# A decode-attention kernel loads V with 64 KB runs, one load per group, and computes its group weights in one block ahead of V's sums

## The chip, the cores and the metric

The kernel runs on one core of one Trainium2 chip. The metric is the device time of one execution in microseconds (us). Times below are medians of all runs of one kernel, with the lowest and the highest in brackets. A run is labelled slow when it lies more than 1.5% above the fastest of its kernel, and fast otherwise; ratios of times use fast runs alone. The profile is one execution; its span is some 1.5 us shorter than the measured time, and all moments in it count from the span's start.

## The reference

Two attention layers, A and B, each decode one token. Both have 32 query heads, 16 key/value heads and a head size of 128. A looks at the last 2048 positions of its cache, B at all 8192. The two outputs are concatenated.

```python
W = min(4096, max(256, Sk // 4))              # A: 2048 of 8192 positions; B uses all
q = (x @ wq).reshape(B, Sq, Hq, Dh)           # x is 1 x 576
scores = einsum("bhqd,bhkd->bhqk", q, k) * Dh ** -0.5
p = softmax(scores); o = einsum("bhqk,bhkd->bhqd", p, v)
out = o.reshape(B, Sq, Hq * Dh) @ wo
```

Every cache row and every weight is read once and used for one token. The input that must be moved is 102.8 MB.

## The kernel before

The work is cut into five groups: group 0 is all of A, groups 1 to 4 are four key/value heads of B each. On-chip memory has four slots of 4 MB, two for K and two for V. One engine (SyncE) issues all large loads in order, each after the work that last used its slot. The loads are carried out by 16 DMA engines, in packets; a packet here is one partition's contiguous run of memory (the packet records hold 2048 packets of 32 KB for B's K and V, 64 MB). TensorE does the matrix products, VectorE elementwise work and reductions, ScalarE the exponential. TensorE runs the groups in one hardware loop: it turns K by transposes, multiplies it with q, turns the softmax numerators P, and multiplies them with V.

V comes in two loads of two heads. Even and odd partitions hold different heads, and each partition's run of memory is 128 rows of 256 bytes, 32 KB:

```python
def load_kv(arrs, g, s, off, res, name):
    dst = slots[:, off:off + SLOT]
    def go(sp):
        if g:                                  # B: groups 1 to 4
            i = 4 * (g - 1) + 2 * s            # two heads
            return sp.dma_start(dst, arrs[1][0, i:i + 2, :, :].rearrange("e (p t) d -> p e (t d)", t=128))
        ...                                    # A: four loads with 8 KB runs
```

P is written twice next to each other by the exponential (for the two heads), turned, and masked by parity:

```python
# exponential: 512 scores -> 1024 columns
src = bass.AP(tensor=sacc, offset=0, ap=[[512, 128], [1, 512], [0, 2]])
act.activation(psb[:, :].rearrange("p (x g) -> p x g", g=2), src, ACT.Exp, bias=..., scale=SCALE, accum_out=...)
# turn: 8 transposes of 128 columns; then two masked copies of 512 columns on VectorE
for e in range(2):
    dve.tensor_scalar(to_e, turned_e, par2[:, e:e + 1], None, ALU.mult)
```

Each group then has 32 matmuls per V slot. In the last group, the chain that finds the weights of all groups (maximum, exponential, totals, scaling, combination; a ping-pong of TensorE, VectorE and ScalarE) stands between quarters of these sums:

```python
softmax_transpose(g, 18)
if last: weights_top(g)
v_slot(g, 0, 0, 20)
if last: weights_exp(g)
v_slot(g, 0, 1, 20.2)
if last: weights_sum(g)
v_keep(g, 0)
v_slot(g, 1, 0, 21)
if last: combine(range(NG - 1), ...); o_columns(0)
v_slot(g, 1, 1, 21.5)
v_keep(g, 1)
```

After the loop, the output weights of A (4.6 MB) and B (in four pieces, the last three in V's place) are multiplied with the result.

Of the kernel before, what the change touches and what calls it, by code (L numbers as in the profile page):

```python
# [12 lines left out]
DH = 128  # L13
# [5 lines left out]
NG = 5  # L19
# [17 lines left out]
class Program:  # L37
# [94 lines left out]
    def waits_of_loop(self, ops):  # L132
# [9 lines left out]
        for key, places in points.items():  # L142
# [26 lines left out]
            if len(fixed) == len(places):  # L169
                for place, hi in fixed.items():  # L170
# [4 lines left out]
                   for n in (1, 2, 16, 64) for first in (0, n) if fits(first, n, some, taker)]  # L175
# [100 lines left out]
def bass_concat_heads__sliding_block_cached__gqa_block_cached__decode_kernel(  # L276
# [24 lines left out]

    prog = Program(nc)
# [4 lines left out]
    ptm = nc.alloc_sbuf_tensor("ptm", [128, 1024], BF16)  # L307
    psb = nc.alloc_sbuf_tensor("psb", [128, 1024], BF16)
# [14 lines left out]
    maskV = nc.alloc_sbuf_tensor("maskV", [128, 8], F32)  # L323
# [3 lines left out]
    wlast = nc.alloc_sbuf_tensor("wlast", [128, 8], F32)  # L327
    vtmp = nc.alloc_sbuf_tensor("vtmp", [128, 8, DH], F32)
# [8 lines left out]
    opsum = nc.alloc_psum_tensor("opsum", [128, 1024], F32)  # L337
# [3 lines left out]
    B_O = [("bank", 5), ("bank", 6)]  # L341
    B_M = ("bank", 7)

# [3 lines left out]
    VS = [[("v", 0, 0), ("v", 0, 1)], [("v", 1)]]  # L347
    koff = lambda s: s * SLOT
    voff = lambda s: (2 + s) * SLOT
# [44 lines left out]
    def load_kv(arrs, g, s, off, res, name):  # L394
        dst = slots[:, off:off + SLOT]

        def go(sp):
            if g:
                i = 4 * (g - 1) + 2 * s
                return sp.dma_start(dst, arrs[1][0, i:i + 2, :, :].rearrange("e (p t) d -> p e (t d)", t=128))  # L400
            for m in range(4):
                i = 4 * m + 2 * s
                src = arrs[0][0, i:i + 2, SK - W_A:, :].rearrange("e (p t) d -> p e (t d)", t=32)
                ins = sp.dma_start(dst[:, m * UNIT:(m + 1) * UNIT], src)
                if m < 3:
                    op.also.append((16, ins))
            return ins
        op = add("sp", go, writes=res, dma="%s%d" % (name, s), inc=64)
# [19 lines left out]
    def q_part(P, off, res):  # L428
        def mm(pe):
            for u in range(9):  # L430
                for j in range(4):
                    o = off + u * 2048 + j * 512
                    ins = pe.matmul(opsum[32 * j:32 * j + 32, P * 512:(P + 1) * 512], lhsT=xpad[:, P, u, :],  # L433
                                    rhs=slots[:, o:o + 512], start=(u == 0), stop=(u == 8))
            return ins
        add("pe", mm, reads=[("xpad", P)] + res, writes=[B_O[P]])

    def q_finish(P):
        add("act", lambda act: act.activation(qrow[:, :], opsum[:, P * 512:(P + 1) * 512], ACT.Copy),  # L439
            reads=[B_O[P]], writes=["qrow"])  # L440

# [63 lines left out]
    def softmax_exp(g):  # L505
# [6 lines left out]
        def go(act):  # L512
            src = bass.AP(tensor=sacc, offset=0, ap=[[512, 128], [1, 512], [0, 2]])
            return act.activation(psb[:, :].rearrange("p (x g) -> p x g", g=2), src, ACT.Exp, bias=st(C_NB + g),  # L514
                                  scale=SCALE, accum_out=st(C_L + g))
# [3 lines left out]
    def softmax_transpose(g, place):  # L519
        dst = misc[:, :].bitcast(BF16)  # L520

        def tr(pe):
            for t in range(8):
                ins = pe.matmul(dst[:, t * 128:(t + 1) * 128], lhsT=psb[:, t * 128:(t + 1) * 128], rhs=ident[:, :],  # L524
                                start=True, stop=True, is_transpose=True)
            return ins
        add("pe", tr, reads=["psb", "ident"], writes=[B_M], loop=(g, place, None))

        def put(dve):
            for e in range(2):  # L530
                to = ptm[:, :].rearrange("p (n e y) -> p n e y", e=2, y=2)[:, :, e, :]
                src = dst.rearrange("p (n e y) -> p n e y", e=2, y=2)[:, :, e, :]
                ins = dve.tensor_scalar(to, src, par2[:, e:e + 1], None, ALU.mult)  # L533
            return ins
        add("dve", put, reads=[B_M, "par2"], writes=["ptm"], tag="put")


    def v_slot(g, s, half, place):
        v = slots[:, voff(s):voff(s) + SLOT].rearrange("p (m y) -> p m y", m=4)

        def mm(pe):
            for tt in range(4 * half, 4 * half + 4):
                for j in range(4):
                    o = tt * 128 + 32 * j
                    b = (8 * j + tt) * 128
                    ins = pe.matmul(opsum[32 * j:32 * j + 32, s * 512:(s + 1) * 512], lhsT=ptm[:, o:o + 32],  # L546
                                    rhs=v[:, :, b:b + 128], start=(tt == 0), stop=(tt == 7), skip_group_check=True)
            return ins
        add("pe", mm, reads=["ptm"] + VS[s], writes=[B_O[s]], loop=(g, place, None))


    def v_keep(g, s):
        last = g == NG - 1
        w = "wlast" if last else "maskV"
        by = bass.AP(tensor=wlast if last else maskV, offset=4 * s, ap=[[8, 128], [1, 4], [0, DH]])
        src = opsum[:, s * 512:(s + 1) * 512].rearrange("p (m d) -> p m d", m=4)
        add("dve", lambda dve: dve.tensor_tensor(vtmp[:, 4 * s:4 * s + 4, :], src, by, ALU.mult),  # L557
            reads=[B_O[s], w], writes=[("vtmp", s)], tag="keep")
        if s:
            sums((accs if last else acc)[:, g, :], vtmp[:, :, :].rearrange("p m d -> p d m"), [("vtmp", 0), ("vtmp", 1)],  # L560
                 [("accs" if last else "acc", g)], "keep")
# [4 lines left out]
    def weights_top(g):  # L566
        def turn(pe):
            pe.matmul(misc[0:1, 0:128], lhsT=st(C_M), rhs=identf[:, :], start=True, stop=True)  # L568
            return pe.matmul(misc[0:4, 128:256], lhsT=st(C_M + 1, 4), rhs=identf[:, :], start=True, stop=True)  # L569
# [181 lines left out]
```

## Time and profile before

| | before |
|---|---|
| time, us | 246.96 (246.78 to 247.31, 6 runs) |
| span of the profiled run, us | 245.4 |
| large loads (queue 1), packets | 5628 |
| sum of packet times, over 16 engines, us | 241.09 |
| packets of 8 KB, of 32 KB: mean time, ns | 313.4, 1217.8 |
| TensorE busy | 67% |

The lines below are from the page of the kernel before. The first four divide the span into 40 slices: the busy share of TensorE in tenths, its granted clock in tenths of full speed, the busy share of the DMA engines, and what they moved. The last line is the queue of the large loads: packets, MB, and the share of 16 engines' span that the packets took.

```profile
PE   0006329993836999443999390999671699859684
...
PEclk9999957999575999795899866599979599975679
DMA  9998999999999999999999999999999999999993
GB/s 349 421 445 383 426 425 421 418 418 419 469 419 433 438 423 427 427 438 427 427 434 443 438 433 433 427 427 427 433 433 427 433 438 433 427 445 427 403 416 140
...
q1 hardware_dynamic: 5628, 102.77, 98.2%
```

The DMA engines are busy almost throughout, while TensorE has gaps in every group. The kernel is bound by its loads (102.87 MB at a mean of 419 GB/s over the span). In the packet records, one packet follows another on an engine without a gap, from 1.0 us to the last weights.

These are the last pieces of the chain that ended last in the kernel before (start, length, what):

```profile
223.79 0.33 SPq L391
224.12 0.04 issue
224.16 18.52 DMA slots<-in_B_wo_dram
...
242.72 0.64 PE ktps L640 x16
...
243.39 0.31 DVE outsb L648
```

The 18.5 us are not a slow load: it is the wait in a full queue. After the last landing only 16 matmuls, a copy and the store are left.

This is TensorE and its helpers in the last group, from the timeline of the kernel before (start, length, engine, line, operation; in brackets the idle time before it and what ended it):

```profile
192.10 5.96 PE L472 MATMUL ktps<-ident,slots 128*128 128x128 bf16 x64 [6.88 <-PEq L214]
...
213.73 0.64 PE L493 MATMUL sacc<-kt,qst 128*32 128x512 bf16 x8 [0.37 <-PEq L214]
...
217.32 0.88 DVE L533 TENSOR_SCALAR ptm<-misc,par 128x512 bf16<-128x512 bf16 x2 [2.03 <-PE misc L524]
...
229.22 1.87 PE L546 MATMUL opsum<-slots,ptm 128*32 128x512 bf16 x13
...
231.86 1.87 DVE L384 TENSOR_REDUCE accs<-vtmp 128x128 f32<-128x1024 f32 x1
...
234.07 6.95 PE L640 MATMUL ktps<-slots,opj 128*32 128x288 bf16 x146
...
241.67 0.62 PE L640 MATMUL ktps<-slots,opj 128*32 128x144 bf16 x28 [0.65 <-DMA slots<-in_B_wo_dram]
242.72 0.61 PE L640 MATMUL ktps<-slots,opj 128*32 128x144 bf16 x16 [0.43 <-DMA slots<-in_B_wo_dram]
```

K's first half lands at 192.1; the last scores end at 214.4, V's sums at 231.1, and TensorE reaches the output weights of B only 0.65 us before their next piece lands. So in this run the tail of TensorE was nearly as late as the loads.

### The profile page before, as it was taken

What the parts mean: (1) busy time and instruction counts of PE and PEld (TensorE: products, weight loads), DVE (VectorE), ACT (ScalarE), POOL (GpSimd) and SP (SyncE); (2) the same over time, 40 slices, a digit from 0 to 9 for tenths busy, and PEclk for the clock granted to TensorE, in tenths of its full rate; (3) what the DMA queues carried; (4) which work ended last, traced back from release to release, by engine and by line L of the source; (5) the groups of instructions that cost most, each with busy time, mean ns of one, the idle gap of its engine ahead of it and who ended that gap; (6) DMA issues with size and microseconds to landing.
All of it is one profiled execution on the core that took longest, in us unless ns stands there. A gap on an engine that the chain in (4) does not pass through costs nothing. (4 is left out here: it accounts for less than half of the span.)

```text
span 245.4 us, 5175 instructions
## 1 busy us (share of the span) xinstructions
PE 165.1 (67%) x2285; PEld 117.5 (48%) x2285; DVE 87.2 (36%) x148; ACT 87.4 (36%) x95; POOL 10.7 (4%) x48
## 2 busy tenths in 40 slices
PE   0006329993836999443999390999671699859684
PEld 0002129781316876213877130978330687625463
DVE  0001205654142465250556323355524256533311
ACT  2000016873003786101778200577600378610000
POOL 7400000000000000000000000000000000000000
PEclk9999957999575999795899866599979599975679
DMA  9998999999999999999999999999999999999993
GB/s 349 421 445 383 426 425 421 418 418 419 469 419 433 438 423 427 427 438 427 427 434 443 438 433 433 427 427 427 433 433 427 433 438 433 427 445 427 403 416 140
DMA packets 5796, 102.87 MB, mean 419 GB/s; under 512 B 794, under 2 KB 924, under 8 KB 1180
## 3 DMA queue, kind: packets, MB, share of 16 engines
q1 hardware_dynamic: 5628, 102.77, 98.2%
q8 instruction: 5, 0.08, 0.1%
q10 hardware_dynamic: 160, 0.00, 0.0%
q14 instruction: 3, 0.02, 0.0%
HBM read 102.76 MB, written 0.00 MB: 419 GB/s over the span
## 5 line engine op out<-in xcount | busy, mean ns | idle before, releaser
L478 ACT ACTIVATE kt<-ktps 128x1024 bf16<-128x1024 bf16 x80 | 78.5, 1022 | 95.1 <-PE ktps L472 94.9
L472 PE MATMUL ktps<-ident,slots 128*128 128x128 bf16 x1280 | 89.1, 236 | 34.1 <-PEq L214 34.1
L472 PEld LDWEIGHTS ktps<-ident,slots 128*128 128x128 bf16 x1280 | 83.2, 107 | 49.7 <-issue 49.7
L481 DVE COPY kt<-ktps 128x1024 bf16<-128x1024 bf16 x80 | 55.3, 692 | 74.1 <-PE ktps L472 74.1
L546 PE MATMUL opsum<-slots,ptm 128*32 128x512 bf16 x320 | 32.0, 557 | 5.1 <-PEq L214 5.1
L493 PE MATMUL sacc<-kt,qst 128*32 128x512 bf16 x320 | 25.4, 392 | 1.9 <-PEq L214 1.9
L546 PEld LDWEIGHTS opsum<-slots,ptm 128*32 128x32 bf16 x320 | 13.0, 127 | 18.9 <-issue 16.8
L557 DVE TENSOR_TENSOR vtmp<-opsum,maskV 128x512 f32<-128x512 f32 x8 | 5.5, 692 | 22.6 <-PE opsum L546 22.6
L415 PE MATMUL misc<-xnine,twice 64*128 64x18 bf16 x1 | 0.2, 173 | 17.8 <-DMA xnine<-in_B_x_dram 17.8
L524 PE MATMUL misc<-ident,psb 128*128 128x128 bf16 x40 | 3.3, 230 | 11.6 <-PEq L214 11.6
L462 POOL COPY qst<-qcol 128x8 bf16<-128x8 bf16 x20 | 3.1, 191 | 163.7 <-PE sacc L493 149.3
L439 ACT ACTIVATE qrow<-opsum 128x512 bf16<-128x512 f32 x2 | 1.2, 597 | 22.7 <-PE opsum L433 22.7
L524 PEld LDWEIGHTS misc<-ident,psb 128*128 128x128 bf16 x40 | 2.5, 101 | 14.0 <-issue 14.0
L640 PE MATMUL ktps<-slots,opj 128*32 128x144 bf16 (+1 forms) x192 | 8.3, 271 | 1.1 <-DMA slots<-in_B_wo_dram 1.1
L514 ACT ACTIVATE psb<-sacc,stat 128x1024 bf16<-128x1024 f32 x5 | 5.6, 1114 | 9.5 <-DVE stat L508 9.5
L493 PEld LDWEIGHTS sacc<-kt,qst 128*32 128x32 bf16 x320 | 5.0, 94 | 7.9 <-issue 4.3
L415 PEld LDWEIGHTS misc<-xnine,twice 64*128 64x128 bf16 x1 | 0.1, 103 | 17.8 <-issue 17.8
L533 DVE TENSOR_SCALAR ptm<-misc,par 128x512 bf16<-128x512 bf16 x10 | 4.4, 480 | 10.4 <-PE misc L524 10.4
L640 PEld LDWEIGHTS ktps<-slots,opj 128*32 128x32 bf16 x192 | 6.2, 104 | 3.1 <-DMA slots<-in_B_wo_dram 1.5
L384 DVE TENSOR_REDUCE acc<-vtmp 128x128 f32<-128x1024 f32 x4 | 7.5, 1872 | 0.1
L433 PE MATMUL opsum<-slots,xpad 128*32 128x512 bf16 x72 | 6.2, 504 | 1.7 <-DMA slots<-in_B_wq_dram 0.9
L424 DVE TENSOR_SCALAR xpad<-misc,par 128x5 bf16<-128x5 f32 (+1 forms) x8 | 1.2, 230 | 14.0 <-PE misc L415 14.0
(65 smaller groups left out, 41.2 us busy)
## 6 DMA issues: line engine op xcount, KB each, us to landing
slots<-in_B_k_cache_dram SPq DMA_DIRECT2D x8, 4096.0 KB
slots<-in_B_v_cache_dram SPq DMA_DIRECT2D x8, 4096.0 KB
slots<-in_A_k_cache_dram SPq DMA_DIRECT2D x8, 1024.0 KB
slots<-in_A_v_cache_dram SPq DMA_DIRECT2D x8, 1024.0 KB
slots<-in_A_wq_dram SPq DMA_DIRECT2D x1, 4608.0 KB, 13.6
slots<-in_B_wq_dram SPq DMA_DIRECT2D x1, 4608.0 KB, 23.7
slots<-in_A_wo_dram SPq DMA_DIRECT2D x1, 4608.0 KB, 19.2
slots<-in_B_wo_dram SPq DMA_DIRECT2D x1, 3024.0 KB, 26.0
```

The lines of the kernel that those rows point to most:

```text
L384: add("dve", lambda dve: dve.tensor_reduce(out, view, AX.X, ALU.add), reads=reads, writes=writes, tag=tag)
L433: ins = pe.matmul(opsum[32 * j:32 * j + 32, P * 512:(P + 1) * 512], lhsT=xpad[:, P, u, :], rhs=slots[:, o:o + 512], start=(u == 0), stop=( ...
L472: ins = pe.matmul(ktps_bf[q][:, t * 128:(t + 1) * 128], lhsT=slots[:, o:o + 128], rhs=ident[:, :], start=True, stop=True, is_transpose=True)
L478: add("act", lambda act, q=q, dst=dst: act.activation(dst, ktps_bf[q], ACT.Copy), reads=[("bank", q)], writes=[("kt", u % NKT, q)], tag="e ...
L481: add("dve", lambda dve, q=q, dst=dst: dve.tensor_copy(dst, ktps_bf[q]), reads=[("bank", q)], writes=[("kt", u % NKT, q)], tag="e%d%d" % ( ...
L493: ins = pe.matmul(sacc[32 * j:32 * j + 32, :], lhsT=qst[:, o:o + 32], rhs=rhs, start=(u == 0 and e == 0), stop=True, skip_group_check=True)
L514: return act.activation(psb[:, :].rearrange("p (x g) -> p x g", g=2), src, ACT.Exp, bias=st(C_NB + g), scale=SCALE, accum_out=st(C_L + g))
L524: ins = pe.matmul(dst[:, t * 128:(t + 1) * 128], lhsT=psb[:, t * 128:(t + 1) * 128], rhs=ident[:, :], start=True, stop=True, is_transpose= ...
L533: ins = dve.tensor_scalar(to, src, par2[:, e:e + 1], None, ALU.mult)
L546: ins = pe.matmul(opsum[32 * j:32 * j + 32, s * 512:(s + 1) * 512], lhsT=ptm[:, o:o + 32], rhs=v[:, :, b:b + 128], start=(tt == 0), stop=( ...
L557: add("dve", lambda dve: dve.tensor_tensor(vtmp[:, 4 * s:4 * s + 4, :], src, by, ALU.mult), reads=[B_O[s], w], writes=[("vtmp", s)], tag=" ...
L640: ins = pe.matmul(ktps[P][32 * j:32 * j + 32, 0:w], lhsT=opj[:, P, jj:jj + 32], rhs=slots[:, o:o + w], start=(jj == 0), stop=(jj == HQ - 1))
```

## The change

The intent is longer packets. V of four heads comes in one 8 MB load, with partition 4p+h holding 256 rows of head h, a run of 64 KB. For this, P has to be spread over four heads instead of two and sorted by even and odd rows of K, which doubles P: the exponential writes 2048 columns, 16 transposes turn them, and two masked copies of 1024 columns follow. V's 64 sums run as one block into one bank, and what is kept afterwards is half as large. The weights chain of the last group goes, as one block, ahead of V's sums. A's V still has packets of 8 KB.

```diff
+    def load_v(g):
+        dst = slots[:, VOFF:VOFF + 2 * SLOT]
+        def go(sp):
+            if g:
+                return sp.dma_start(dst, vs[1][0, 4 * g - 4:4 * g, :, :].rearrange("h (p t) d -> p h (t d)", t=256))
+            for i in range(8):                                    # A
+                m, c = divmod(i, 2)
+                src = vs[0][0, 4 * m:4 * m + 4, SK - W_A:, :].rearrange("h (p c t) d -> p h c (t d)", c=2, t=32)[:, :, c, :]
 ...
-            src = bass.AP(tensor=sacc, offset=0, ap=[[512, 128], [1, 512], [0, 2]])
+            src = bass.AP(tensor=sacc, offset=0, ap=[[512, 128], [2, 256], [1, 2], [0, 4]])
+            dst = bass.AP(tensor=psb, offset=0, ap=[[2048, 128], [4, 256], [1024, 2], [1, 4]])
 ...
+            return dve.tensor_tensor(ptm[:, c * 1024:(c + 1) * 1024]..., dst..., mask, ALU.mult)   # once per c
 ...
+            for c in range(2):
+                for tt in range(8):
+                    for j in range(4):
+                        o = c * 1024 + tt * 128 + 32 * j
+                        b = (8 * j + tt) * 128
+                        ins = pe.matmul(opsum[32 * j:32 * j + 32, :], lhsT=ptm[:, o:o + 32], rhs=v[:, c, :, b:b + 128],
+                                        start=(c == 0 and tt == 0), stop=(c == 1 and tt == 7), skip_group_check=True)
 ...
-        (weights_top, v_slot, weights_exp, v_slot, weights_sum, v_keep, v_slot, combine, v_slot, v_keep)
+        for c in range(2):
+            softmax_transpose(g, c, 18 + c / 2)
+        if g == NG - 1:
+            weights_top(g)
+            weights_exp(g)
+            weights_sum(g)
+            combine(range(NG - 1), (g, 19.3, LAST))
+            o_columns(0)
+        v_sums(g, 20)
+        v_keep(g)
```

(Cut; the line in brackets abridges the removed order.)

More of the change, by code (lines that the diff above doesn't have):

```diff
@@ L174, in waits_of_loop @@
             fit = [(first, n, some, taker) for some in (places, also) for taker in sorted(some, key=lambda p: (-runs[p], -p))
-                   for n in (1, 2, 16, 64) for first in (0, n) if fits(first, n, some, taker)]
+                   for n in (1, 2, 16, 64, 128) for first in (0, n) if fits(first, n, some, taker)]
             assert fit, (key, places, [(p, k.get(key, 0), w.get(key)) for p, k, w in state if p in places])
@@ L306, in bass_concat_heads__sliding_block_cached__gqa_block_cached__decode_kernel @@
     kt = nc.alloc_sbuf_tensor("kt", [128, NKT, UNIT], BF16)
-    ptm = nc.alloc_sbuf_tensor("ptm", [128, 1024], BF16)
-    psb = nc.alloc_sbuf_tensor("psb", [128, 1024], BF16)
+    ptm = nc.alloc_sbuf_tensor("ptm", [128, 2048], BF16)
+    psb = nc.alloc_sbuf_tensor("psb", [128, 2048], BF16)
     ident = nc.alloc_sbuf_tensor("ident", [128, 128], BF16)
@@ L322, in bass_concat_heads__sliding_block_cached__gqa_block_cached__decode_kernel @@
     par2 = nc.alloc_sbuf_tensor("par2", [128, 2], F32)
-    maskV = nc.alloc_sbuf_tensor("maskV", [128, 8], F32)
+    maskV = nc.alloc_sbuf_tensor("maskV", [128, 4], F32)
+    four = nc.alloc_sbuf_tensor("four", [128, 4], F32)
+    maskP = nc.alloc_sbuf_tensor("maskP", [128, 128], BF16)
     qrow = nc.alloc_sbuf_tensor("qrow", [128, 512], BF16)
@@ L326, in bass_concat_heads__sliding_block_cached__gqa_block_cached__decode_kernel @@
     srow = nc.alloc_sbuf_tensor("srow", [4, 2, 160], F32)
-    wlast = nc.alloc_sbuf_tensor("wlast", [128, 8], F32)
-    vtmp = nc.alloc_sbuf_tensor("vtmp", [128, 8, DH], F32)
+    wlast = nc.alloc_sbuf_tensor("wlast", [128, 4], F32)
+    vtmp = nc.alloc_sbuf_tensor("vtmp", [128, 4, DH], F32)
     acc = nc.alloc_sbuf_tensor("acc", [128, NG, DH], F32)
@@ L336, in bass_concat_heads__sliding_block_cached__gqa_block_cached__decode_kernel @@
     sacc = nc.alloc_psum_tensor("sacc", [128, 512], F32)
-    opsum = nc.alloc_psum_tensor("opsum", [128, 1024], F32)
+    opsum = nc.alloc_psum_tensor("opsum", [128, 512], F32)
+    turned = nc.alloc_psum_tensor("turned", [128, 512], F32)
     misc = nc.alloc_psum_tensor("misc", [128, 512], F32)
@@ L340, in bass_concat_heads__sliding_block_cached__gqa_block_cached__decode_kernel @@
     B_S = ("bank", 4)
-    B_O = [("bank", 5), ("bank", 6)]
+    B_O = ("bank", 5)
+    B_T = ("bank", 6)
     B_M = ("bank", 7)
+    wsum, B_W = ktps[3], ("bank", 3)
     KS = [[("k", 0)], [("k", 1, 0), ("k", 1, 1)]]
-    VS = [[("v", 0, 0), ("v", 0, 1)], [("v", 1)]]
+    VS = [("v", 0), ("v", 1), ("v", 2)]
     koff = lambda s: s * SLOT
-    voff = lambda s: (2 + s) * SLOT
+    VOFF = 2 * SLOT
     def load_x(P):
@@ L391, in load, with load_k @@
         add("sp", lambda sp: sp.dma_start(dst, src()), writes=writes, dma=dma)
-    def load_kv(arrs, g, s, off, res, name):
-        dst = slots[:, off:off + SLOT]
+    def load_k(g, s):
+        dst = slots[:, koff(s):koff(s) + SLOT]
         def go(sp):
@@ L399, in go @@
                 i = 4 * (g - 1) + 2 * s
-                return sp.dma_start(dst, arrs[1][0, i:i + 2, :, :].rearrange("e (p t) d -> p e (t d)", t=128))
+                return sp.dma_start(dst, ks[1][0, i:i + 2, :, :].rearrange("e (p t) d -> p e (t d)", t=128))
             for m in range(4):
                 i = 4 * m + 2 * s
-                src = arrs[0][0, i:i + 2, SK - W_A:, :].rearrange("e (p t) d -> p e (t d)", t=32)
+                src = ks[0][0, i:i + 2, SK - W_A:, :].rearrange("e (p t) d -> p e (t d)", t=32)
                 ins = sp.dma_start(dst[:, m * UNIT:(m + 1) * UNIT], src)
@@ L407, in go @@
             return ins
-        op = add("sp", go, writes=res, dma="%s%d" % (name, s), inc=64)
+        op = add("sp", go, writes=KS[s], dma="k%d" % s, inc=64)
+    def load_v(g):
[6 more added lines that the diff above has]
+                src = vs[0][0, 4 * m:4 * m + 4, SK - W_A:, :].rearrange("h (p c t) d -> p h c (t d)", c=2, t=32)[:, :, c, :]
+                o = (4 * c + m) * UNIT
+                ins = sp.dma_start(dst[:, o:o + UNIT], src)
+                if i < 7:
+                    op.also.append((16, ins))
+            return ins
+        op = add("sp", go, writes=VS, dma="v", inc=128)
     add("dve", lambda dve: dve.tensor_copy(twice[:, :].rearrange("p (m e) -> p m e", e=2),
@@ L432, in mm @@
                     o = off + u * 2048 + j * 512
-                    ins = pe.matmul(opsum[32 * j:32 * j + 32, P * 512:(P + 1) * 512], lhsT=xpad[:, P, u, :],
+                    ins = pe.matmul((turned if P else opsum)[32 * j:32 * j + 32, :], lhsT=xpad[:, P, u, :],
                                     rhs=slots[:, o:o + 512], start=(u == 0), stop=(u == 8))
             return ins
-        add("pe", mm, reads=[("xpad", P)] + res, writes=[B_O[P]])
+        add("pe", mm, reads=[("xpad", P)] + res, writes=[B_T if P else B_O])
     def q_finish(P):
-        add("act", lambda act: act.activation(qrow[:, :], opsum[:, P * 512:(P + 1) * 512], ACT.Copy),
-            reads=[B_O[P]], writes=["qrow"])
+        add("act", lambda act: act.activation(qrow[:, :], (turned if P else opsum)[:, :], ACT.Copy),
+            reads=[B_T if P else B_O], writes=["qrow"])
         def tr(pe):
@@ L512, in go @@
         def go(act):
-            src = bass.AP(tensor=sacc, offset=0, ap=[[512, 128], [1, 512], [0, 2]])
-            return act.activation(psb[:, :].rearrange("p (x g) -> p x g", g=2), src, ACT.Exp, bias=st(C_NB + g),
-                                  scale=SCALE, accum_out=st(C_L + g))
+            src = bass.AP(tensor=sacc, offset=0, ap=[[512, 128], [2, 256], [1, 2], [0, 4]])
+            dst = bass.AP(tensor=psb, offset=0, ap=[[2048, 128], [4, 256], [1024, 2], [1, 4]])
+            return act.activation(dst, src, ACT.Exp, bias=st(C_NB + g), scale=SCALE, accum_out=st(C_L + g))
@@ L516, in softmax_exp, with softmax_transpose @@
         add("act", go, reads=[B_S, ("st", C_NB + g)], writes=["psb", ("st", C_L + g)], tag="exp")
-    def softmax_transpose(g, place):
-        dst = misc[:, :].bitcast(BF16)
+    def softmax_transpose(g, c, place):
+        bank, res = ((misc, B_M), (turned, B_T))[c]
+        dst = bank[:, :].bitcast(BF16)
         def tr(pe):
             for t in range(8):
-                ins = pe.matmul(dst[:, t * 128:(t + 1) * 128], lhsT=psb[:, t * 128:(t + 1) * 128], rhs=ident[:, :],
+                o = c * 1024 + t * 128
+                ins = pe.matmul(dst[:, t * 128:(t + 1) * 128], lhsT=psb[:, o:o + 128], rhs=ident[:, :],
@@ L525, in tr @@
                                 start=True, stop=True, is_transpose=True)
             return ins
-        add("pe", tr, reads=["psb", "ident"], writes=[B_M], loop=(g, place, None))
+        add("pe", tr, reads=["psb", "ident"], writes=[res], loop=(g, place, None))
         def put(dve):
-            for e in range(2):
-                to = ptm[:, :].rearrange("p (n e y) -> p n e y", e=2, y=2)[:, :, e, :]
-                src = dst.rearrange("p (n e y) -> p n e y", e=2, y=2)[:, :, e, :]
-                ins = dve.tensor_scalar(to, src, par2[:, e:e + 1], None, ALU.mult)
-            return ins
@@ L535, in softmax_transpose @@
-        add("dve", put, reads=[B_M, "par2"], writes=["ptm"], tag="put")
-    def v_slot(g, s, half, place):
-        v = slots[:, voff(s):voff(s) + SLOT].rearrange("p (m y) -> p m y", m=4)
-        def mm(pe):
-            for tt in range(4 * half, 4 * half + 4):
-                for j in range(4):
-                    o = tt * 128 + 32 * j
-                    b = (8 * j + tt) * 128
-                    ins = pe.matmul(opsum[32 * j:32 * j + 32, s * 512:(s + 1) * 512], lhsT=ptm[:, o:o + 32],
-                                    rhs=v[:, :, b:b + 128], start=(tt == 0), stop=(tt == 7), skip_group_check=True)
-            return ins
-        add("pe", mm, reads=["ptm"] + VS[s], writes=[B_O[s]], loop=(g, place, None))
@@ L552, in v_keep, with v_sums, mm @@
-    def v_keep(g, s):
+            mask = bass.AP(tensor=maskP, offset=0, ap=[[128, 128], [0, 8], [1, 128]])
+            return dve.tensor_tensor(ptm[:, c * 1024:(c + 1) * 1024].rearrange("p (t y) -> p t y", t=8),
+                                     dst.rearrange("p (t y) -> p t y", t=8), mask, ALU.mult)
+        add("dve", put, reads=[res, "maskP"], writes=[("ptm", c)], tag="put%d" % c)
+    def v_sums(g, place):
+        v = slots[:, VOFF:VOFF + 2 * SLOT].rearrange("p (c m y) -> p c m y", c=2, m=4)
+        def mm(pe):
+            for c in range(2):
[5 more added lines that the diff above has]
+                                        start=(c == 0 and tt == 0), stop=(c == 1 and tt == 7), skip_group_check=True)
+            return ins
+        add("pe", mm, reads=[("ptm", 0), ("ptm", 1)] + VS, writes=[B_O], loop=(g, place, None))
@@ L553, in v_keep @@
+    def v_keep(g):
         last = g == NG - 1
         w = "wlast" if last else "maskV"
-        by = bass.AP(tensor=wlast if last else maskV, offset=4 * s, ap=[[8, 128], [1, 4], [0, DH]])
-        src = opsum[:, s * 512:(s + 1) * 512].rearrange("p (m d) -> p m d", m=4)
-        add("dve", lambda dve: dve.tensor_tensor(vtmp[:, 4 * s:4 * s + 4, :], src, by, ALU.mult),
-            reads=[B_O[s], w], writes=[("vtmp", s)], tag="keep")
-        if s:
-            sums((accs if last else acc)[:, g, :], vtmp[:, :, :].rearrange("p m d -> p d m"), [("vtmp", 0), ("vtmp", 1)],
-                 [("accs" if last else "acc", g)], "keep")
+        by = bass.AP(tensor=wlast if last else maskV, offset=0, ap=[[4, 128], [1, 4], [0, DH]])
+        src = opsum[:, :].rearrange("p (m d) -> p m d", m=4)
+        add("dve", lambda dve: dve.tensor_tensor(vtmp[:, :, :], src, by, ALU.mult),
+            reads=[B_O, w], writes=["vtmp"], tag="keep")
+        sums((accs if last else acc)[:, g, :], vtmp[:, :, :].rearrange("p m d -> p d m"), ["vtmp"],
+             [("accs" if last else "acc", g)], "keep")
@@ L567, in turn @@
         def turn(pe):
-            pe.matmul(misc[0:1, 0:128], lhsT=st(C_M), rhs=identf[:, :], start=True, stop=True)
-            return pe.matmul(misc[0:4, 128:256], lhsT=st(C_M + 1, 4), rhs=identf[:, :], start=True, stop=True)
-        add("pe", turn, reads=[("st", C_M + c) for c in range(NG)] + ["identf"], writes=[B_M], loop=(g, 18.5, LAST))
+            pe.matmul(wsum[0:1, 0:128], lhsT=st(C_M), rhs=identf[:, :], start=True, stop=True)
+            return pe.matmul(wsum[0:4, 128:256], lhsT=st(C_M + 1, 4), rhs=identf[:, :], start=True, stop=True)
+        add("pe", turn, reads=[("st", C_M + c) for c in range(NG)] + ["identf"], writes=[B_W], loop=(g, 19, LAST))
         def top(dve):
-            dve.tensor_reduce(srow[0:1, 0, 0:32], misc[0:1, 0:128].rearrange("p (j h) -> p h j", j=4), AX.X, ALU.max)
-            return dve.tensor_reduce(srow[0:4, 1, 0:8], misc[0:4, 128:256].rearrange("p (a r) -> p r a", r=8),
+            dve.tensor_reduce(srow[0:1, 0, 0:32], wsum[0:1, 0:128].rearrange("p (j h) -> p h j", j=4), AX.X, ALU.max)
+            return dve.tensor_reduce(srow[0:4, 1, 0:8], wsum[0:4, 128:256].rearrange("p (a r) -> p r a", r=8),
                                      AX.X, ALU.max)
-        add("dve", top, reads=[B_M], writes=["srow"])
+        add("dve", top, reads=[B_W], writes=["srow"])
         def rep(dve):
@@ L586, in back @@
         def back(pe):
-            pe.matmul(misc[:, 256:257], lhsT=srow[0:1, 0, 32:160], rhs=onesf[0:1, 0:1], start=True, stop=True)
-            return pe.matmul(misc[:, 257:261], lhsT=srow[0:4, 1, 32:160], rhs=identf[0:4, 0:4], start=True, stop=True)
-        add("pe", back, reads=["srow2", "ones", "identf"], writes=[B_M], loop=(g, 20.1, LAST))
-        add("dve", lambda dve: dve.scalar_tensor_tensor(st(C_T, NG), st(C_M, NG), SCALE, misc[:, 256:261],
+            pe.matmul(wsum[:, 256:257], lhsT=srow[0:1, 0, 32:160], rhs=onesf[0:1, 0:1], start=True, stop=True)
+            return pe.matmul(wsum[:, 257:261], lhsT=srow[0:4, 1, 32:160], rhs=identf[0:4, 0:4], start=True, stop=True)
+        add("pe", back, reads=["srow2", "ones", "identf"], writes=[B_W], loop=(g, 19.1, LAST))
+        add("dve", lambda dve: dve.scalar_tensor_tensor(st(C_T, NG), st(C_M, NG), SCALE, wsum[:, 256:261],
                                                         ALU.mult, ALU.add),
-            reads=[B_M] + [("st", C_M + c) for c in range(NG)], writes=[("st", C_T)])
+            reads=[B_W] + [("st", C_M + c) for c in range(NG)], writes=[("st", C_T)])
         add("act", lambda act: act.activation(st(C_W, NG), st(C_T, NG), ACT.Exp),
@@ L599, in total @@
         def total(pe):
-            pe.matmul(misc[:, 264:265], lhsT=same[:, :], rhs=st(C_T + 5), start=True, stop=True)
-            return pe.matmul(misc[:, 265:269], lhsT=sameB[:, :], rhs=st(C_T + 6, 4), start=True, stop=True)
-        add("pe", total, reads=[("st", C_T + 5), "same", "sameB"], writes=[B_M], loop=(g, 20.3, LAST))
-        add("dve", lambda dve: dve.reciprocal(st(C_T + 10, NG), misc[:, 264:269]),
-            reads=[B_M], writes=[("st", C_T + 10)])
-        add("dve", lambda dve: dve.scalar_tensor_tensor(st(C_AL, NG), st(C_W, NG), 2.0, st(C_T + 10, NG),
+            pe.matmul(wsum[:, 264:265], lhsT=same[:, :], rhs=st(C_T + 5), start=True, stop=True)
+            return pe.matmul(wsum[:, 265:269], lhsT=sameB[:, :], rhs=st(C_T + 6, 4), start=True, stop=True)
+        add("pe", total, reads=[("st", C_T + 5), "same", "sameB"], writes=[B_W], loop=(g, 19.2, LAST))
+        add("dve", lambda dve: dve.reciprocal(st(C_T + 10, NG), wsum[:, 264:269]),
+            reads=[B_W], writes=[("st", C_T + 10)])
+        add("dve", lambda dve: dve.scalar_tensor_tensor(st(C_AL, NG), st(C_W, NG), 4.0, st(C_T + 10, NG),
                                                         ALU.mult, ALU.mult),
@@ L619, in mm @@
                     w = pickB[:, r, :] if g else pick[:, r, :]
-                    to = misc[32 * (g - 1):32 * g, 304:336] if g else misc[:, 272:304]
+                    to = wsum[32 * (g - 1):32 * g, 304:336] if g else wsum[:, 272:304]
                     ins = pe.matmul(to, lhsT=w, rhs=accs[:, g, 32 * r:32 * r + 32], start=(r == 0), stop=(r == 3))
             return ins
-        add("pe", mm, reads=["pick", "pickB"] + [("accs", g) for g in groups], writes=[B_M], loop=loop)
+        add("pe", mm, reads=["pick", "pickB"] + [("accs", g) for g in groups], writes=[B_W], loop=loop)
     def o_columns(P):
-        add("dve", lambda dve: dve.tensor_copy(opj[:, P, 0:32], misc[:, 272 + 32 * P:304 + 32 * P]),
-            reads=[B_M], writes=[("opj", P)])
+        add("dve", lambda dve: dve.tensor_copy(opj[:, P, 0:32], wsum[:, 272 + 32 * P:304 + 32 * P]),
+            reads=[B_W], writes=[("opj", P)])
     def load_wo(P, lo, n, off, res):
@@ L655, in finish_out @@
         add("sp", put, reads=[("outsb", P)], writes=[("out", P)], dma="out%d" % P)
-    WQ = [(4 * SLOT - WQ_W, [("v", 0, 1), ("v", 1)]), (SLOT, [("k", 1, 0), ("k", 1, 1), ("v", 0, 0)])]
+    WQ = [(4 * SLOT - WQ_W, [("v", 2)]), (SLOT, [("k", 1, 0), ("k", 1, 1), ("v", 0)])]
     for P in range(2):
@@ L665, in bass_concat_heads__sliding_block_cached__gqa_block_cached__decode_kernel @@
         q_finish(P)
-    sums(maskV[:, :], same[:, 0:32].rearrange("p (m s y) -> p s m y", m=4, s=2), ["same"], ["maskV"])
+    sums(maskV[:, :], same[:, 0:32].rearrange("p (m y) -> p m y", m=4), ["same"], ["maskV"])
+    sums(four[:, :], ident[:, :].rearrange("p (x h) -> p h x", h=4), ["ident"], ["four"])
+    add("dve", lambda dve: dve.tensor_copy(maskP[:, :].rearrange("p (x h y) -> p x h y", x=16, h=4),
+                                           bass.AP(tensor=four, offset=0, ap=[[4, 128], [0, 16], [1, 4], [0, 2]])),
+        reads=["four"], writes=["maskP"])
     sums(sameB[:, 0:8], same[:, 0:32].rearrange("p (m y) -> p y m", m=4), ["same"], ["sameB0"])
@@ L674, in bass_concat_heads__sliding_block_cached__gqa_block_cached__decode_kernel @@
         for s in range(2):
-            load_kv(ks, g, s, koff(s), KS[s], "k")
-        for s in range(2):
-            load_kv(vs, g, s, voff(s), VS[s], "v")
+            load_k(g, s)
+        load_v(g)
         for s in range(2):
@@ L687, in bass_concat_heads__sliding_block_cached__gqa_block_cached__decode_kernel @@
         softmax_exp(g)
-        softmax_transpose(g, 18)
+        for c in range(2):
+            softmax_transpose(g, c, 18 + c / 2)
         if g == NG - 1:
             weights_top(g)
-        v_slot(g, 0, 0, 20)
-        if g == NG - 1:
             weights_exp(g)
-        v_slot(g, 0, 1, 20.2)
-        if g == NG - 1:
             weights_sum(g)
-        v_keep(g, 0)
-        v_slot(g, 1, 0, 21)
-        if g == NG - 1:
-            combine(range(NG - 1), (g, 21.2, LAST))
+            combine(range(NG - 1), (g, 19.3, LAST))
             o_columns(0)
-        v_slot(g, 1, 1, 21.5)
-        v_keep(g, 1)
+        v_sums(g, 20)
+        v_keep(g)
     wo_loads = [
@@ L707, in bass_concat_heads__sliding_block_cached__gqa_block_cached__decode_kernel @@
         (1, 0, 21, WQ_W, [("k", 1, 1)]),
-        (1, 21, 7, 2 * SLOT, [("v", 0, 0), ("v", 0, 1)]),
+        (1, 21, 7, 2 * SLOT, [("v", 0), ("v", 1)]),
         (1, 28, 3, 2 * SLOT + 7 * DM, [("w", 0)]),
```

## The prediction

> **What bounds the kernel.** The DMA engines. The page's queue table gives queue 1 a 98.2% share of 16 engines' span for 102.77 MB; the DMA row of the slices is 9 nearly throughout, at 416 to 445 GB/s; packet records follow each other without gaps. TensorE is busy 67%, and its idle time is waiting for data. The chain of waits ends with 18.5 us of queued output-weight loads, 16 matmuls, one copy and the store.
>
> **What longer runs save.** In the packet records an 8 KB packet takes 313 ns on average, a 32 KB packet 1218 ns. The difference is 36.8 ps per byte, 435 GB/s over 16 engines[...]; this leaves 11 ns per packet. B's V has 1024 packets of 32 KB; 512 of 64 KB save 512 x 11 ns / 16 = 0.35 us (estimate). A's V keeps 8 KB packets; K and weights are unchanged.
>
> **What moves.** Per group: the exponential writes 2048 columns instead of 1024 (1.11 us now; estimate 2.0), 16 instead of 8 turns of P (+0.6 us), two masked copies of 1024 columns instead of 512 (0.48 us each; estimate 1.2, because the 512-column PSUM multiply in this trace takes 0.69 us). So P is ready about 6.2 us after the last scores instead of 3.9. V is one load, issued after all its sums. In the timeline the sums now run from 102.0 to 106.9, while the next V load is needed at about 121.8 (K of the group in between takes 19.6 us). Ending near 110 leaves over 10 us: no DMA bubble. The reduce of the kept sums halves (1.87 us to about 1.0). None of this is critical, except in the last group.
>
> **The tail.** Before, the weights chain is interleaved with V's sums: last scores 214.4, sums end 231.1, keep and combine to 234.1, first output part to 239.7, second part until it waits for the load at 241.7; slack under 1 us. After: P ready at 220.7, then the whole weights chain (maximum, exponential, totals, scaling, 16 fp32 combines; about 8 us by the timeline's durations), so V's 64 matmuls start near 228.8. At half clock they take 7.2 us (3.6 us per 32), at full half of that. [...]this trace's clock records change at multiples of 3.41 us. [...]I estimate the sums end near 233.6 (232.5 to 236.5), keep and combine end 235.9, the first output part 241.6, the rest 244 instead of 243.3. The last output-weight load is issued when V's sums end; the queue runs dry only at 237.8, so it survives. Tail: +0.7 us, between -0.3 and +4.
>
> **Sum.** 247.0 - 0.35 + 0.75 = 247.4 us, range 246.2 to 249.8. Chances: faster by over 2% 0.01, within 2% 0.95, slower by over 2% 0.04.
>
> **What would show it.** Packet records: 512 of 64 KB at about 2425 ns; queue-1 share and mean rate within 1%; no DMA gap between groups; in the last group V's sums starting near 229, and output matmuls ending near 244, with TensorE rather than the load last in the chain.
>
> **What would make it wrong.** 64 KB packets slower than two of 32 KB; the clock staying at half through the tail (+6 us); the queue running dry before the last weights.

Three passages are cut where marked, because no run here shows what they said. No term of the sum is among them: it came to 247.0 - 0.35 + 0.75 = 247.4 us. Its end of V's sums at 233.6 us, 4.8 us after their start at 228.8, lies between 7.2 us at half clock and 3.6 us at full (in the trace before, 32 sums took 3.60 us at half clock, and 36 started within 2.01 us at full), and rested on the assumption that the clock would rise on the way.

## More of the kernel before

VectorE's groups in the kernel before (line, operation, shapes, count; busy us and mean ns of one):

```profile
L481 DVE COPY kt<-ktps 128x1024 bf16<-128x1024 bf16 x80 | 55.3, 692 | 74.1 <-PE ktps L472 74.1
L557 DVE TENSOR_TENSOR vtmp<-opsum,maskV 128x512 f32<-128x512 f32 x8 | 5.5, 692 | 22.6 <-PE opsum L546 22.6
L533 DVE TENSOR_SCALAR ptm<-misc,par 128x512 bf16<-128x512 bf16 x10 | 4.4, 480 | 10.4 <-PE misc L524 10.4
```

These give the costs from which the change was estimated.

## The result and the profile after

| | before | after |
|---|---|---|
| time, us | 246.96 (246.78 to 247.31) | 246.68 (246.54 to 246.88) |
| span of the profiled run, us | 245.4 | 245.0 |
| queue 1, packets | 5628 | 5052 |
| sum of packet times over 16 engines, us | 241.09 | 240.61 |
| B's V: packets, mean ns | 1024 of 32 KB, 1217.8 (K and V together) | 512 of 64 KB, 2423.6 |

The ratio of times is 0.9989, with a 95% interval of 0.9976 to 1.0002. A ratio is the mean time of one kernel's fast runs over that of the other's fast runs of the same rounds, so it is not quite the ratio of the medians. The change is worth a tenth of a percent, and this pair alone doesn't settle that it isn't zero.

The same lines of the page after:

```profile
PEclk9999857999575999768899857799857999995999
DMA  9999999999999999899999999999989999989993
GB/s 337 434 434 391 424 427 415 420 423 420 464 428 428 508 397 449 375 428 428 481 419 449 401 407 433 439 492 407 471 375 428 439 482 417 449 386 409 432 402 153
...
q1 hardware_dynamic: 5052, 102.77, 98.2%
```

The load engines are as full as before. The rate per slice swings more: from 375 to 508 in the fourth to the 38th slice, against 383 to 469 before. The longer packets go with it: in the changed kernel cut to 32 KB packets (below) it runs from 398 to 456. The last pieces of the chain after:

```profile
229.58 0.33 SPq L398
229.90 0.04 issue
229.95 12.34 DMA slots<-in_B_wo_dram
...
242.33 0.64 PE ktps L665 x16
...
242.99 0.31 DVE outsb L673
```

The end is the same: last weights, 16 matmuls, copy, store, all 0.4 us earlier. The piece is issued 5.8 us later and lands 0.4 us earlier, so the wait before was only the queue. The tail in the timeline after:

```profile
191.79 3.78 PE L495 MATMUL ktps<-ident,slots 128*128 128x128 bf16 x64 [3.88 <-PEq L214]
...
211.76 0.64 PE L516 MATMUL sacc<-kt,qst 128*32 128x512 bf16 x8 [0.37 <-PEq L214]
...
224.51 5.02 PE L572 MATMUL opsum<-slots,ptm 128*32 128x512 bf16 x61
...
230.31 1.02 DVE L391 TENSOR_REDUCE accs<-vtmp 128x128 f32<-128x512 f32 x1
...
231.69 4.10 PE L665 MATMUL ktps<-slots,opj 128*32 128x288 bf16 x64
...
238.84 1.50 PE L665 MATMUL ktps<-slots,opj 128*32 128x144 bf16 x84 [3.06 <-DMA slots<-in_B_wo_dram]
241.27 0.62 PE L665 MATMUL ktps<-slots,opj 128*32 128x144 bf16 x28 [0.93 <-DMA slots<-in_B_wo_dram]
```

TensorE is now done with the first output part at 235.8 and waits 3.1 us for weights. Two things made this tail earlier. The last scores end 2 us earlier than before (212.4 against 214.4): K's half landed 0.3 us earlier, and the first 64 transposes took 3.78 us instead of 5.96, because the granted clock stood at full there, and at half until 196.8 before. Both are readings of one profile each. And the masked copies were cheap, as VectorE's groups after show:

```profile
L558 DVE TENSOR_TENSOR ptm<-misc,maskP 128x1024 bf16<-128x1024 bf16 x5 | 3.5, 692 | 16.0 <-PE misc L551 16.0
L583 DVE TENSOR_TENSOR vtmp<-opsum,maskV 128x512 f32<-128x512 f32 x4 | 2.8, 692 | 30.9 <-PE opsum L572 30.9
```

1024 columns of bf16 take the 692 ns that 512 columns of f32 take.

### The profile page after: what moved, and what is told of

Its sections match the earlier page's. It is cut to its first block, busy times and chain, and to the rows that moved or that the text cites. A ratio compares the mean times of both kernels' runs of the same rounds, so it can differ in the third digit from the quotient of the medians.

```text
span 245.0 us, 5228 instructions
## 1 busy us (share of the span) xinstructions
PE 160.8 (66%) x2325; PEld 117.3 (48%) x2325; DVE 82.3 (34%) x145; ACT 91.1 (37%) x95; POOL 10.7 (4%) x48
## 3 DMA queue, kind: packets, MB, share of 16 engines
q1 hardware_dynamic: 5052, 102.77, 98.2%
## 5 line engine op out<-in xcount | busy, mean ns | idle before, releaser
L495 PE MATMUL ktps<-ident,slots 128*128 128x128 bf16 x1280 | 85.0, 230 | 23.0 <-PEq L214 23.0
L495 PEld LDWEIGHTS ktps<-ident,slots 128*128 128x128 bf16 x1280 | 79.1, 104 | 38.3 <-issue 38.3
L572 PE MATMUL opsum<-slots,ptm 128*32 128x512 bf16 x320 | 28.2, 528 | 10.6 <-PEq L214 10.6
L572 PEld LDWEIGHTS opsum<-slots,ptm 128*32 128x32 bf16 x320 | 13.7, 127 | 23.7 <-issue 21.7
L551 PE MATMUL misc<-ident,psb 128*128 128x128 bf16 x40 | 4.7, 288 | 15.8 <-PEq L214 15.8
L538 ACT ACTIVATE psb<-sacc,stat 128x2048 bf16<-128x2048 f32 x5 | 9.8, 1967 | 9.5 <-DVE stat L531 9.5
L583 DVE TENSOR_TENSOR vtmp<-opsum,maskV 128x512 f32<-128x512 f32 x4 | 2.8, 692 | 30.9 <-PE opsum L572 30.9
L665 PE MATMUL ktps<-slots,opj 128*32 128x144 bf16 (+1 forms) x192 | 6.8, 247 | 4.4 <-DMA slots<-in_B_wo_dram 4.4
L558 DVE TENSOR_TENSOR ptm<-misc,maskP 128x1024 bf16<-128x1024 bf16 x5 | 3.5, 692 | 16.0 <-PE misc L551 16.0
L529 DVE TENSOR_REDUCE stat<-sacc 128x1 f32<-128x512 f32 x5 | 3.5, 692 | 4.5 <-PE sacc L516 4.5
L551 PE MATMUL turned<-ident,psb 128*128 128x128 bf16 x40 | 4.8, 293 | 0.0
```

The costliest lines, as they stand in the source:

```text
L495: ins = pe.matmul(ktps_bf[q][:, t * 128:(t + 1) * 128], lhsT=slots[:, o:o + 128], rhs=ident[:, :], start=True, stop=True, is_transpose=True)
L529: add("dve", lambda dve: dve.tensor_reduce(st(C_M + g), sacc[:, :], AX.X, ALU.max), reads=[B_S], writes=[("st", C_M + g)], tag="max")
L538: return act.activation(dst, src, ACT.Exp, bias=st(C_NB + g), scale=SCALE, accum_out=st(C_L + g))
L551: ins = pe.matmul(dst[:, t * 128:(t + 1) * 128], lhsT=psb[:, o:o + 128], rhs=ident[:, :], start=True, stop=True, is_transpose=True)
L558: return dve.tensor_tensor(ptm[:, c * 1024:(c + 1) * 1024].rearrange("p (t y) -> p t y", t=8), dst.rearrange("p (t y) -> p t y", t=8), mas ...
L572: ins = pe.matmul(opsum[32 * j:32 * j + 32, :], lhsT=ptm[:, o:o + 32], rhs=v[:, c, :, b:b + 128], start=(c == 0 and tt == 0), stop=(c == 1 ...
```

## The experiments

There are three theories. Theory 1: the gain is the fixed cost of a packet, saved 32 times per engine, and all that moved on the other engines is covered by the loads. Theory 2: the gain comes from the new order of the tail. Theory 3: it comes from the pattern of addresses (four heads at a time). Kernels ran beside the kernel before, which took 246.91 to 246.95 us (medians). All experiments gave correct results.

### Shorter packets in the changed kernel

The edit cuts the 8 MB load into n loads of parts of the runs; layout in memory, heads, sums and order stay (n is 2, 4 and 8).

```diff
-    return sp.dma_start(dst, vs[1][0, 4*g-4:4*g, :, :].rearrange("h (p t) d -> p h (t d)", t=256))
+    for i in range(n):
+        src = vs[1][0, 4*g-4:4*g, :, :].rearrange("h (p c t) d -> p h c (t d)", c=n, t=256//n)[:, :, i, :]
+        ins = sp.dma_start(dst[:, i*(32768//n):(i+1)*(32768//n)], src)
+        if i < n - 1: op.also.append((16, ins))
+    return ins
```

> The changed kernel, but each 8 MB load of B's V is cut into 2 loads of half runs: 1024 packets of 32 KB instead of 512 of 64 KB; same heads and rows per partition, same sums, same weights block. Theory 1 (the gain is the fixed cost per packet, 11 ns): back to about the time of the kernel before, 247.0 to 247.1 us. Theory 2 (the gain comes from the order of the tail, weights ahead of V) and theory 3 (it comes from the four-head address pattern): stays at 246.7 us.

> As run32, in 4 loads of 16 KB runs: 2048 packets. Theory 1: 96 more packets per engine than with 64 KB runs, at 11.3 ns: +1.1 us, 247.8 us. Theories 2 and 3: 246.7 us.

> As run32, in 8 loads of 8 KB runs: 4096 packets. Theory 1: eight packets of 313.5 ns against one of 2423.6 ns cost 84 ns more, times 32 per engine: +2.7 us, 249.4 us. Theories 2 and 3: 246.7 us.

| B's V in packets of | packets per engine | mean packet, ns | sum of packet times, us | time, us | ratio to before (95%) |
|---|---|---|---|---|---|
| 64 KB (the change) | 32 | 2423.6 | 240.61 | 246.68 | 0.9989 (0.9976 to 1.0002) |
| 32 KB | 64 | 1217.7 (with K) | 241.08 | 246.98 (246.76 to 247.31) | 0.9998 (0.9984 to 1.0011) |
| 16 KB | 128 | 615.1 | 242.06 | 247.61 (247.39 to 247.63) | 1.0023 (1.0010 to 1.0035) |
| 8 KB | 256 | 313.8 (with A) | 243.69 | 248.80 (248.58 to 249.03) | 1.0073 (1.0059 to 1.0086) |

The time follows the number of packets. Against 64 KB it grows by 0.30, 0.93 and 2.12 us for 32, 96 and 224 more packets per engine: 9.4, 9.7 and 9.5 ns for each. With 32 KB packets the changed kernel is back at the time of the kernel before, although its tail and its address pattern are the new ones. Theory 1 holds; theories 2 and 3, which expected 246.7 us in all three, find no support: by them the 32 KB run would have stayed 0.2 us under the kernel before, and it did not. The step from 64 to 32 KB is not clear of noise by itself (the intervals overlap); the steps to 16 and 8 KB are.

These edits change the number of loads along with the packets (4, 12 and 28 more loads of V, some 76 ns each), so the times alone can't tell a cost per packet from a cost per load. The packet records can: in the 8 KB run nine in ten of B's V packets took between 309 and 321 ns, so it is not a few slow packets at the start of a load, and eight packets of the median 313 ns take 82 ns more than one of the median 2422 ns.

The 8 KB run was expected at 249.4 us and came 0.6 us lower. By the durations of the packets, one more packet costs about 12 ns (two of 32 KB against one of 64 KB: 2435.4 - 2423.6; eight of 8 KB: 2510.4 - 2423.6, over 7), so a fifth of that did not reach the total. The records account for it, in one trace each: packets on an engine overlap slightly, and more when they are short. Between 1 and 240 us, 16.02 packets were in flight on average with 64 KB packets and 16.09 with 8 KB, on 16 engines. The sums of packet times divided by this overlap differ by 2.1 us, as the times do (2.12).

### The weights chain back between the sums

```diff
         if g == NG - 1:
             weights_top(g)
+        v_sums(g, 20, 0, 4)        # a quarter of the 64 sums
+        if g == NG - 1:
             weights_exp(g)
+        v_sums(g, 20.2, 4, 8)
+        if g == NG - 1:
             weights_sum(g)
+        v_sums(g, 21, 8, 12)
+        if g == NG - 1:
             combine(range(NG - 1), (g, 21.2, LAST))
             o_columns(0)
-        v_sums(g, 20)
+        v_sums(g, 21.5, 12, 16)
```

(Cut here and in the diffs below: the changed arguments of `v_sums` and `v_slot`, and the new places of the chain's steps in the loop.)

> The changed kernel with the weights chain again cut between four quarters of V's sums in the last group, as before the change. Theory 1: TensorE still ends before the last weights land, so the same time as the changed kernel, 246.7 us, within 0.2. Theory 2: the gain is lost, 247.0 us.

It took 247.06 us, ratio 0.9996 (0.9979 to 1.0013). Its fastest run, 246.52 us, equals the fastest of the changed kernel (246.54), but its runs spread up to 247.78, and those of the changed kernel only up to 246.88. The profiled run is the slowest. These are the sums of two stretches in it, from the last scores to the combination and from there to the end (length; busy us and instruction count of each engine; granted clock, DMA share, GB/s):

```profile
213.70:235.10 21.40, 14.52 (x124) 8.48 (x124) 6.64 (x20) 2.27 (x3) 0.00 (x0) 0.58 0.98 421
235.10:246.30 11.20, 9.15 (x200) 6.74 (x200) 0.95 (x3) 0.00 (x0) 0.00 (x0) 0.73 0.51 211
```

And the same two stretches in the profiled run of the changed kernel:

```profile
212.40:231.40 19.00, 10.61 (x125) 8.88 (x125) 6.46 (x20) 2.27 (x3) 0.00 (x0) 0.82 0.97 418
231.40:245.00 13.60, 7.11 (x200) 5.46 (x200) 0.95 (x3) 0.00 (x0) 0.00 (x0) 0.98 0.70 291
```

The same instructions kept TensorE busy 23.7 us at a granted clock of 0.58 and 0.73, and 17.7 us at 0.82 and 0.98. In the interleaved run the output matmuls ran without a wait for data and ended at 244.3, after the last weights: there TensorE was the end of the chain.

One part of this tail is not the clock. The last packet of V's single 8 MB load ended at 220.4 in the interleaved run and 220.3 in the changed kernel. In the interleaved order the first quarter of the sums has to wait for it, and the rest of the weights chain stands behind that quarter:

```profile
221.24 1.90 PE L573 MATMUL opsum<-slots,ptm 128*32 128x512 bf16 x16 [1.90 <-PEq L214]
```

TensorE stood idle for 1.9 us. (The trace names only TensorE's own sequencer; that V is what it waits for is inferred from the packets.) The block order runs the chain in this time, and its sums start only at 224.3. In the kernel before, the packets of V's first 4 MB ended at about 210.3, and the sums started at 218.5. So the one large load is a reason for the block order.

Whether the order matters is not settled: two of the six runs were as fast as the changed kernel, and the profiled one, the slowest, took 1.1 us more than the median of the changed kernel. Whether the order itself brings the low clock is tried below, and stays open.

### How much slack the tail has

V's sums are done again in the last group alone, ahead of the real ones, which overwrite them; 32, 64 and 128 extra matmuls.

```diff
+        if g == NG - 1:
+            v_sums(g, 19.9, LAST, 8)     # 8: 32 extra sums; 16: 64; 32: 128
         v_sums(g, 20)
```

> The changed kernel with 32 extra sums in the last group, d = 1.8 to 3.6 us: inside the slack of about 3 to 4 us. Expected 246.7 us, at most 247.0. With a slack under 1 us: 248 us or more.

> The changed kernel with V's 64 sums done twice in the last group only (the second overwrites the first, so the result stays right). They add d = 3.4 (full clock) to 5 us to the tail on TensorE. My reading of the changed kernel's timeline is a slack there of 3.1 us to the first wait for output weights and about 4 us in all. Expected: 246.7 to 247.7 us. If the tail were critical as the prediction had it (slack under 1 us), 249 to 251 us.

> As tail64 with 128 extra sums, d = 7 to 9 us. Beyond the slack of 4 us: 249.5 to 252 us, with TensorE instead of the last load ending last. If only the DMA queue mattered and the tail never, 246.7 us.

> tail128 again, on the chip of the other two: about 250.9 us.

| extra sums | time, us | ratio to before (95%) |
|---|---|---|
| 32 | 246.71 (246.60 to 248.12) | 1.0003 (0.9982 to 1.0023) |
| 64 | 247.96 (247.10 to 249.03) | 1.0053 (1.0015 to 1.0092) |
| 128 | 250.94 (248.79 to 251.79) | 1.0145 (1.0088 to 1.0202) |
| 128, other chip | 251.01 (250.83 to 252.65) | 1.0175 (1.0149 to 1.0202) |

With 32 extra sums, four of six runs (246.60 to 246.72) don't notice them; two do. With 64 the time begins to move, two of four runs by only 0.4 us. With 128, TensorE ends last. So the tail of the changed kernel has a slack of about 3 us, as its timeline shows, where the prediction had TensorE ending last, with no slack at all (its "under 1 us" was that of the kernel before). The two longer runs of the 64 (248.8 and 249.0 us) lie beyond the expectation, and runs of one kernel here differ by up to 3 us once TensorE is the end, where the load-bound kernels agree within 1.1 us. The clock is the obvious suspect, but of the runs that were not profiled the record has only its mean over the whole run, and that does not follow the time: the longest run with 32 extra sums (248.12 us) and the shortest with 128 on the first chip (248.79 us) both have the highest mean of their kernel, 0.869.

These are the extra and the real sums, and the output matmuls, in the timeline of the second run with 128:

```profile
226.32 12.76 PE L573 MATMUL opsum<-slots,ptm 128*32 128x512 bf16 x189
...
241.22 6.20 PE L666 MATMUL ktps<-slots,opj 128*32 128x288 bf16 x190
```

The 190 output matmuls run through without one wait for weights, and the span is 249.5 us.

### More work in the loop

```diff
+        if g < NG - 1:
+            v_sums(g, 19.9, (lambda g: g < NG - 1), 16)
         v_sums(g, 20)
```

> The changed kernel with V's 64 sums done twice in the first four groups, not in the last: about 4 x 5 us more TensorE work in the loop, and V's buffer is released 5 us later in each. The prediction says over 10 us of margin before the DMA queue runs dry: 246.7 us, within 0.3. If TensorE or V's later release bounded the loop: up to +20 us.

It took 246.63 us (246.48 to 246.78), ratio 0.9987 (0.9970 to 1.0003): the same as the changed kernel, with 256 more matmuls and a later release of V in each of four groups. Neither TensorE nor the release of V's 8 MB bounds the loop. The doubled P, which costs 0.9 us more of exponential and 0.6 us more of transposes per group, is therefore covered too.

### Which tail is shorter: not settled

The same 128 extra sums were put into the kernel before, and into the interleaved kernel, once ahead of its first quarter and once behind its last.

```diff
 # kernel before: four times the first half of V, ahead of its own sums
+            v_slot(g, 0, 0, 19.9, LAST, 4)
         v_slot(g, 0, 0, 20)
 # interleaved kernel, ahead (first run) or behind (second run)
+            v_sums(g, 19.9, 0, 32, LAST)
         v_sums(g, 20, 0, 4)
 ...
         v_sums(g, 21.5, 12, 16)
+            v_sums(g, 22, 0, 32, LAST)
```

> The kernel before with 128 extra sums in the last group (V's first half four times over, ahead of its own sums, overwritten by them), which makes TensorE the end of the chain; so its time reads the length of its tail. The prediction's sums say that its tail is 0.7 us shorter than that of the changed kernel: then 0.7 us under tail128b. The two timelines, from the last scores to the last output column, say 19.4 us against 18.9: then the same within 0.5 us, about 250.5 us.

> The interleaved kernel with the same 128 extra sums ahead of V's first quarter. If the block of weights ahead of V shortens the tail, as the timelines say (21.4 us against 18.9 in the profiled runs, part of it clock), it is 1 to 2.5 us slower than tail128b. If the order of the tail does not matter: the same within 0.5 us.

> The interleaved kernel with the 128 extra sums behind V's last quarter instead of ahead of the first, so that they can't fill the waits of the weights chain[...]. In tail128b, too, they stand behind the whole chain, so this differs from it by the order of the weights chain alone (and by chance of the clock). If the order matters as in the profiled runs of interleaved and of the changed kernel (21.4 us against 19.0 from the last scores to the last combine): 1 to 2.5 us over tail128b, 252 to 253.5 us. If the 3.4 us by which interleaved128 was faster than tail128b came from the order of the chain and not from where the extra sums stood: 247.6 us again.

The kernel before took 249.35 us (247.08 to 251.65, one of them labelled slow; the five fast ones have a median of 248.84), neither of the two times expected. The interleaved kernel with the sums ahead took 247.61 us (247.23 to 252.95, the last labelled slow), 3.4 us less than the block order with as many extra sums, where it was expected to be slower: a miss. In both kernels the extra sums stood ahead of most of the weights chain, so they were not a plain addition. This is their line in the interleaved kernel:

```profile
220.97 8.30 PE L573 MATMUL opsum<-slots,ptm 128*32 128x512 bf16 x144 [0.48 <-DMA slots<-in_B_v_cache_dram]
```

144 sums took 8.3 us here, 58 ns each, against 68 ns each in the line above (12.76 us for 189), and the clock records of this run stand at full from 221.7 to the end; in the run of the block order they stand at half from 213.8 to 230.9. Over the stretch from the last scores to the combination the granted clock was 0.92 in the interleaved run and 0.70 in that of the block order. That the extra sums filled waits of the weights chain would fit the shorter time, but no run separates it from the clock, and what set the clock is not shown.

With the extra sums behind the last quarter, the six runs lie between 247.30 and 253.40 us, with a median of 252.07. Four of them count as slow by the rule of 1.5% over the fastest run; the two others are 247.3 and 248.8. The median is in the range expected for "the order costs", but comparing fast runs alone would say the reverse, so this decides nothing. Its profiled run, a slow one, shows the wait for V again: TensorE stood idle for 3.87 us until 221.2. With the tail bound by TensorE, the spread between runs (6 us) is larger than the difference sought.

## Why the prediction was right or wrong

The time was in the range, and the same within 2%. The centre, 247.4 us, was 0.7 us too high.

- "The DMA engines" bound the kernel: right. The queue's share is 98.2% in both, and 256 more matmuls in the loop cost nothing.
- "0.35 us" for longer packets: right in mechanism and nearly in size. A 64 KB packet took 2423.6 ns where 2425 was said. B's V took 77.56 us of packet time per engine, where B's K in the same run (the same bytes in 32 KB packets) took 77.92, so 0.36 us; the measured time fell by 0.28, and 32 KB packets in the changed kernel gave 0.30 back. Neither difference is clear of noise by itself; the series of packet lengths carries the reading.
- "no DMA bubble" in the loop: right.
- "+0.75" in the sum, for the tail: this step failed. It measured zero, within the noise. The tail was said to end TensorE at 244 with TensorE last in the chain; in the profile the last output matmuls started at 242.33, released by the load. Its parts: P was ready at 217.5 and not 220.7, of which 2 us are the earlier last scores (clock and landing) and about 1 us the masked copies (0.69 us each, not 1.2); the weights block took 7.2 us instead of 8; the sums took 5.3 us, about as said; the first output part took 4.1 us at full clock instead of 5.7. Together they left TensorE 3.1 us of slack where none was forecast. The stated range held a tail that costs nothing as well as one that costs 3 us, so that the time fell into it says nothing for this step.
- "the queue running dry before the last weights" did not happen: V's sums ended at 229.6, and the packets queued before lasted to 238.4.

The error about the masked copies had a source: I took the rate of the f32 multiply from the trace for a bf16 one (in the traces 692 ns for 512 columns of f32, and 692 ns for 1024 of bf16). The error about the clock could not be avoided from one profile: in the traces here the clock of the same instructions stands at half in one run and at full in another (the first 64 transposes of the last group: 5.96 us, at half until 196.8, and 3.78 us, at full). What makes it rise is not shown.

## What to carry to other kernels

In this kernel, whose load engines hardly pause (98.2% of the span), the time followed the packets: some 9.5 ns for each packet on an engine, between 8 and 64 KB. Counted this way, going from 32 to 64 KB for V is worth 0.3 us of 247, which the pair of kernels alone does not tell from zero. Work that was doubled on other engines was free while it fitted under the loads, but look at the tail separately, where the order of the engines can surface and runs differed by microseconds (fast runs of the kernel before with 128 extra sums: 247.08 to 250.46 us), with the clock of TensorE as a suspect and not as a shown cause. Where one large load takes the place of two, work that needs only its first half has to wait for the whole (1.9 us here): put other work there. An experiment that adds work must also ask where the added work stands, because it may do more than add its own length (128 sums: 4.3 us in one place, 0.6 in another, against their own kernels).
